# Moving each chunk's down projection ahead of the next drive in a fused scan and feed-forward kernel, with new budgets for the scan steps

## Chip, cores, metric

One core of one Trainium2 chip. The metric is device time in microseconds; "span" is the time from the first to the last traced instruction of the core, and it is a little shorter than the time. The granted TensorE clock is the share of full speed that the throttle let through, mean over the span. The kernel before takes 190.05 us (median of four runs, 189.99 to 190.41).

Short names: PE is TensorE, DVE is VectorE, ACT is ScalarE, POOL is GpSimd.

## The reference

For 2048 tokens of width 448: a layernorm; a diagonal complex state-space recurrence on the normalized tokens (branch A); a gated feed-forward with 1792 hidden units (branch B); and a gated sum.

```python
xn = layernorm(x)
# A: Bu = xn @ B_bar;  h_t = Lam_bar * h_{t-1} + Bu_t;  s = 2 Re(h @ C^T) + xn * Dskip
# B: B(xn) = (silu(xn @ w_gate) * (xn @ w_up)) @ w_down
g = silu(B(xn))
out = x + s * g
```

## The kernel before

The tokens go in four chunks of 512. For a chunk q, PE runs four stages:

- **drive**: input products of the scan (`pb`), pairs of matmuls on half the rows each;
- **gate/up** (`gu`): seven steps of four accumulations, also half-row pairs;
- **down**: four groups of 14 full-row matmuls (`hd`), from the product tile `Vt`;
- **outputs** (`outs`): four groups of C times the state `H` (`y`), then on DVE the gate, the sum and the store.

All PSUM results take turns in eight banks. The scan of a chunk is 19 DVE steps (six rotations in, seven scans, six rotations back) and one ACT copy. They wait in a background queue, and `bg.run(budget)` lets some of them into DVE's program between other work:

```python
    def run(self, budget):
        self.credit = min(self.credit + budget, 2.0 * budget)
        while self.steps and self.credit > 0:
            _, cost, fn = self.steps.popleft()
            fn()
            self.credit -= cost
```

The order of stages at the end of the kernel before:

```python
    drive(1, 4.8)
    for q in range(NQ - 1):
        sg = []
        for j in range(TQ):
            sg.append(down(q, j))
            bg.run(2.2)
        bg.finish(q)
        for j in range(TQ):
            finish(q, j, out_sum(q, j), sg[j])
        if q + 2 < NQ:
            drive(q + 2, 4.0)
            # ...
            gu(q + 2, bg, 2.2 if last else 1.5, {...})   # layernorm of chunk q+3 rides along
    # ... the last chunk: down and outputs, the last tile in two halves
```

A gate/up step hands a notice through POOL between the two halves of each accumulation (`tell`), and the square root of the layernorm is a POOL power that runs between such notices (`run_power`).

Of the kernel before, what the change touches and what calls it, by code (L numbers as in the profile page):

```python
# [44 lines left out]
def kernel(  # L45
# [25 lines left out]
    NQ = L // W  # L71
# [325 lines left out]
    def bu_alloc(q):  # L397
        bu_of[q] = [
            work.tile([P, KT, W], BF16, name=f"bu_{c}") for c in ("re", "im")
        ]  # L400
# [37 lines left out]
    def bu(q, ns, packed=False):  # L438

        C1 = W // 2  # L440
        b0, b1 = bu_of[q]
        ns = [*ns, KF] if packed else ns
        for two in (ns[:2], ns[2:]):
            pairs = []
            for n in two:
                pb = [bank("pb") for _ in range(2)]
                if n < KF:
                    pairs.append([(pb[i][:], BT[:, :, block(m)], (0, W))
                                  for i, m in enumerate((n, KT + n))])
                else:  # L450
                    pairs.append([(pb[i][:, 0:C1], BT[:, :, block(KF)], (i * C1, i * C1 + C1))
                                  for i in range(2)])
            if pairs:
                sums(q, pairs)
            for n, pair in zip(two, pairs):
                for i in range(2):
                    to = bu_of[q][i][:, n, :] if n < KF else b0[:, KF, i * C1 : i * C1 + C1]
                    nc.scalar.activation(to, pair[i][0], ACT.Copy)  # L458
        if packed:
            turn_over(b1[:, KF, :], b0[:, KF, :])  # L460
# [8 lines left out]
    def ssm_steps(bg, q):  # L469
        T = {}  # L470

        def alloc():
            T["b"] = bu_of[q]
            T["e"] = [work.tile([P, KT - c, W], BF16, name=n, bufs=1)
                      for c, n in enumerate(("ere", "eim"))]
            T["t"] = work.tile([P, KT, W], BF16, name="tmp", bufs=1)
            T["h"] = H_of[q] = [work.tile([P, KT - c, W], BF16, name=n)
                                for c, n in enumerate(("H_re", "H_im"))]

        def of(z, n):  # L480
            z = T["t"] if z == "t" else T[z[0]][z[1]] if isinstance(z, tuple) else z
            return z[:, 0:n, :]

        def step(n, out, a, b, op):
            def run():
                if not T:
                    alloc()
                nc.vector.tensor_tensor(out=of(out, n), in0=of(a, n), in1=of(b, n), op=op)

            bg.add(q, 0.3 * n, run)  # L490

        def scan(k, c):
            init = 0.0 if q == 0 else H_of[q - 1][c][:, k, W - 1 : W]
            nc.vector.tensor_tensor_scan(  # L494
                out=T["b"][c][:, k, :], data0=rcol[:, k : k + 1].to_broadcast([P, W]),
                data1=T["e"][c][:, k, :], initial=init, op0=ALU.mult, op1=ALU.add,
            )

        b0, b1, e0, e1, h0, h1 = (z for n in "beh" for z in ((n, 0), (n, 1)))
        step(KT, e0, b0, CT, ALU.mult)  # L500
        step(KT, "t", b1, ST, ALU.mult)
        step(KT, e0, e0, "t", ALU.add)
        step(KF, e1, b1, CT, ALU.mult)
        step(KF, "t", b0, ST, ALU.mult)
        step(KF, e1, e1, "t", ALU.subtract)
        for k in range(KF, -1, -1):
            for c in range(2 if k < KF else 1):
                bg.add(q, 1.22, lambda k=k, c=c: scan(k, c))
        bg.add(q, 0.0, lambda: turn_over(T["b"][1][:, KF, :], T["b"][0][:, KF, :]))
        step(KF, h1, b1, CT, ALU.mult)  # L510
        step(KF, "t", b0, ST, ALU.mult)
        step(KF, h1, h1, "t", ALU.add)
        step(KT, h0, b0, CT, ALU.mult)
        step(KT, "t", b1, ST, ALU.mult)
        step(KT, h0, h0, "t", ALU.subtract)
# [14 lines left out]
    def gu(q, bg, budget, hooks={}, begun=None):  # L530

        Vt = big.tile([P, NF, W], BF16, name="Vt", tag="vt")
        Vt_of[q] = Vt
        for f0 in range(0, NF, GRP):
            n = min(GRP, NF - f0)
            gs = work.tile([P, GRP, W], BF16, name="gs")
            us = work.tile([P, GRP, W], BF16, name="us")
            for i in range(0, n, 2):
                fi = f0 + i
                if begun and fi == 0:  # L540
                    banks = begun
                else:
                    banks = gu_banks()
                    gu_matmuls(q, fi, banks, 0, W)
                for j, (gp_, up_) in enumerate(banks):
                    nc.scalar.activation(gs[:, i + j, :], gp_[:], ACT.Silu)  # L546
                    nc.scalar.activation(us[:, i + j, :], up_[:], ACT.Copy)  # L547
                for fn in hooks.get(fi // 2, ()):
                    fn()
                bg.run(budget)  # L550
            nc.vector.tensor_tensor(  # L551
                out=Vt[:, f0 : f0 + n, :], in0=gs[:, 0:n, :], in1=us[:, 0:n, :], op=ALU.mult
            )

    def down(q, j):

        hd = bank("hd")[:, 0:D]
        for fi in range(NF):
            nc.tensor.matmul(  # L559
                hd, lhsT=Vt_of[q][:, fi, j * P : (j + 1) * P], rhs=Wd[:, fi, :],  # L560
                start=(fi == 0), stop=(fi == NF - 1),
            )
        sg = work.tile([P, D], BF16, name="sg", bufs=TQ)
        nc.scalar.activation(sg[:], hd, ACT.Silu)  # L564
        return sg

    def out_sum(q, j, k0=0, k1=KT):

        y = bank("y")
        m = q * TQ + j  # L570
        c0, c1 = k0 * P, min(k1 * P, D)
        for n in range(NS):
            h = H_of[q][n // KT][:, n % KT, j * P : (j + 1) * P]
            nc.tensor.matmul(  # L574
                y[:, c0:c1], lhsT=h, rhs=C2[:, n, c0:c1], start=(n == 0), stop=(n == NS - 1)
            )
            if k0 <= n < k1:
                skip = 0 if n < KF else P - R
                s = blk(n).start
                nc.tensor.matmul(  # L580
                    y[:, s + skip : s + P], lhsT=xT[:, n, m * P : (m + 1) * P],
                    rhs=Dd[:, n, skip:P], start=False, stop=False,
                )
        return y[:, c0:c1]

    def finish(q, j, y, sg, eng=nc.sync, c0=0, c1=D):
        m = q * TQ + j
        of = dict(tag="scr_f") if c1 - c0 < D else dict(bufs=1)
        t = work.tile([P, c1 - c0], F32, name="t", **of)
        nc.vector.tensor_tensor(out=t[:], in0=y, in1=sg[:, c0:c1], op=ALU.mult)  # L590
        of = dict(tag="scr_a") if c1 - c0 < D else {}
        ob = work.tile([P, c1 - c0], BF16, name="ob", **of)
        nc.vector.tensor_tensor(out=ob[:], in0=t[:], in1=x_all[:, m, c0:c1], op=ALU.add)  # L593
        eng.dma_start(out=out2d[m * P : (m + 1) * P, c0:c1], in_=ob[:])
# [57 lines left out]
    def load_c():  # L652
# [9 lines left out]
        4: [on(params_trig), on(ssm_steps, bg, 0)],  # L662
        5: [on(params_out)],
    }, begun)
    gu(1, bg, 0.9, {
        1: stats(8, 9),
        2: [*stats(10, 11), *sqrt(2), on(c_weights, 0)],
# [2 lines left out]
        5: [*transposes(10, 11), on(c_weights, 3)],  # L670
    })

    def drive(q, budget):
        bu_alloc(q)
        bu(q, (0, 1, 2), True)
        ssm_steps(bg, q)
        bg.run(budget)

    drive(1, 4.8)
    for q in range(NQ - 1):  # L680
        sg = []
        for j in range(TQ):
            sg.append(down(q, j))
            bg.run(2.2)
        bg.finish(q)
        for j in range(TQ):
            finish(q, j, out_sum(q, j), sg[j])
        if q + 2 < NQ:
            drive(q + 2, 4.0)
            n = (q + 3) * TQ  # L690
            last = q + 3 == NQ
            gu(q + 2, bg, 2.2 if last else 1.5, {} if last else {
                0: stats(n, n + 1),
                1: stats(n + 2, n + 3) + sqrt(q + 3),
                2: rstd_of(q + 3) + norms(n, n + 1),
                3: norms(n + 2, n + 3) + transposes(n, n + 1),
                4: transposes(n + 2, n + 3),
            })
    q, last = NQ - 1, TQ - 1
    bg.finish(q)  # L700
    sg = [down(q, j) for j in range(last)]
    for j in range(last):
        finish(q, j, out_sum(q, j), sg[j])
    sg = down(q, last)
    for k0, k1, eng in ((0, 2, nc.sync), (2, KT, nc.scalar)):
        finish(q, last, out_sum(q, last, k0, k1), sg, eng, k0 * P, min(k1 * P, D))
# [1 line left out]
_INS = ['A_x', 'A_Lambda_re', 'A_Lambda_im', 'A_B_re', 'A_B_im', 'A_C_re', 'A_C_im', 'A_log_dt', 'A_Dskip', 'B_x', 'B_w_gate', 'B_w_up', 'B_w_down']  # L708
_OUTS = [((1, 2048, 448), 'bfloat16')]
# [25 lines left out]
```

## Time and profile before

| | |
|---|---|
| time | 190.05 us |
| span | 188.1 us |
| PE busy | 182.1 us (97%) |
| DVE busy | 160.3 us (85%) |
| ACT busy | 105.1 us (56%) |
| chain that ended last | 84% PE |

The lines themselves stand in the prediction below. The two questions to put to them are whether PE streams at its rate or only looks busy, and which engine makes it wait.

### The profile page before, as it was taken

The numbers are of one execution on the slowest core, as the hardware profiler recorded it, in microseconds if no ns is written. First come the engines' busy times: TensorE is split into PE (matmuls) and PEld (weight loads), VectorE is DVE, ScalarE is ACT, GpSimd is POOL, SyncE is SP. The second block draws the span as 40 slices with busy tenths as digits, with TensorE's granted clock in tenths as the row PEclk, the third lists the DMA queues.
The fourth block names the chain that finished last, engine by engine and source line by source line (L and its number), as shares of the span: only waits on it lengthen the run. The fifth ranks groups of instructions, "written<-read, shape, count | busy, mean of one in ns | idle before, by whom it ended". The sixth has DMA issues, their size and how long they took to land.

```text
span 188.1 us, 3787 instructions
## 1 busy us (share of the span) xinstructions
PE 182.1 (97%) x1512; PEld 93.9 (50%) x1512; DVE 160.3 (85%) x266; ACT 105.1 (56%) x201; POOL 11.2 (6%) x21
## 2 busy tenths in 40 slices
PE   7799999999999999999999999999999999999992
PEld 2575455555555555545444455545444445555551
DVE  4889995899999999989999899789369999789253
ACT  3278699939999871018878632108977552302100
POOL 6422100000020000000020000000000000000000
PEclk9999999999999999999999999999999999999999
DMA  5999997300012100011004000020000000020020
GB/s 152 340 378 383 378 177 144 74 3 2 3 28 56 31 0 0 0 54 51 0 3 97 14 3 0 3 84 15 2 0 3 0 0 0 3 73 24 0 78 24
DMA packets 21122, 12.61 MB, mean 67 GB/s; under 512 B 11120, under 2 KB 20080, under 8 KB 21104
## 3 DMA queue, kind: packets, MB, share of 16 engines
q1 hardware_dynamic: 20288, 12.05, 23.2%
q10 hardware_dynamic: 688, 0.31, 0.6%
q8 instruction: 12, 0.20, 0.5%
q14 instruction: 6, 0.05, 0.1%
q0 software_dynamic: 128, 0.00, 0.0%
HBM read 8.03 MB, written 1.84 MB: 52 GB/s over the span
## 4 chain that ended last, share of the span: by engine, by line
PE 84%; DVE 9%; ACT 3%; DMA 1%; issue 1%; POOL 0%; SPq 0%; DVEq 0%
PE hd L559 23%; PE gp L424 20%; PE up L424 19%; PE y L574 11%; PE pb L424 9%; PE y L580 2%; DVE st L230 1%; DMA x_all<-in_A_x_dram 1%; DVE xn L248 1%; DVE f L356 1%; DVE a L357 1%; ACT CT L306 1%; DVE Vt L551 1%; ACT bu_im L458 1%; ACT bu_re L458 1%; DVE mv L231 1%
## 5 line engine op out<-in xcount | busy, mean ns | idle before, releaser
L424 PE MATMUL gp<-xT,Wg 64*128 64x512 bf16 (+1 forms) x406 | 86.2, 369 | 0.1
L424 PE MATMUL up<-xT,Wu 64*128 64x512 bf16 (+1 forms) x406 | 85.8, 369 | 0.1
L424 PEld LDWEIGHTS <-Wg 64*128 64x128 bf16 x406 | 36.9, 94 | 23.0 <-issue 1.6
L424 PEld LDWEIGHTS <-Wu 64*128 64x128 bf16 x406 | 37.2, 94 | 20.1 <-POOLq L406 0.3
L559 PE MATMUL hd<-Wd,Vt 128*128 128x448 bf16 x224 | 43.2, 353 | 0.0
L546 ACT ACTIVATE gs<-gp 128x512 bf16<-128x512 f32 x56 | 34.9, 623 | 12.4 <-PE gp L424 9.0
L547 ACT ACTIVATE us<-up 128x512 bf16<-128x512 f32 x56 | 35.2, 629 | 0.0
L559 PEld LDWEIGHTS <-Vt 128*128 128x128 bf16 x224 | 21.7, 98 | 21.0 <-issue 1.1
L564 ACT ACTIVATE sg<-hd 128x448 bf16<-128x448 f32 x16 | 8.7, 544 | 38.2 <-PE hd L559 38.2
L424 PE MATMUL pb<-xT,BT 64*128 64x512 bf16 (+1 forms) x224 | 22.0, 349 | 0.0
L551 DVE TENSOR_TENSOR Vt<-gs,us 128x2048 bf16<-128x2048 bf16 (+1 forms) x16 | 17.3, 1081 | 5.5 <-ACT us L547 5.4
L458 ACT ACTIVATE bu_re<-pb 128x512 bf16<-128x512 f32 (+1 forms) x20 | 10.0, 526 | 18.1 <-PE pb L424 18.1
L590 DVE TENSOR_TENSOR t<-y,sg 128x448 f32<-128x448 f32 (+2 forms) x17 | 10.1, 595 | 10.4 <-PE y L574 10.0
L574 PE MATMUL y<-C,H_re 128*128 128x448 bf16 (+2 forms) x68 | 17.6, 341 | 0.0
L424 PEld LDWEIGHTS <-BT 64*128 64x128 bf16 x224 | 11.2, 94 | 11.0 <-issue 0.7
L494 DVE TENSOR_TENSOR_SCAN bu_re<-rcol,H_re,ere 128x512 bf16<-128x512 f32 x12 | 15.1, 1269 | 0.0
L580 PE MATMUL y<-Dd,xT 128*128 128x128 bf16 x64 | 13.5, 212 | 0.0
L574 PE MATMUL y<-C,H_im 128*128 128x448 bf16 (+2 forms) x51 | 11.9, 342 | 0.0
L494 DVE TENSOR_TENSOR_SCAN bu_im<-rcol,H_im,eim 128x512 bf16<-128x512 f32 x9 | 11.3, 1260 | 0.0
L230 DVE BATCH_NORM_STATS2 st<-x_all 128x6 f32<-128x448 bf16 x16 | 9.9, 616 | 1.6 <-DMA x_all<-in_A_x_dram 1.5
L593 DVE TENSOR_TENSOR ob<-t,x_all 128x448 bf16<-128x448 f32 (+2 forms) x17 | 10.2, 597 | 0.6
L215 POOL TENSOR_TENSOR sd<-vep,halves 128x1 bf16<-128x1 bf16 (+1 forms) x7 | 5.9, 845 | 77.0 <-PE up L424 41.6
(90 smaller groups left out, 166.6 us busy)
## 6 DMA issues: line engine op xcount, KB each, us to landing
out_dram<-ob SPq DMA_DIRECT2D x15, 112.0 KB, 1.7
Wd<-in_B_w_down_dram SPq DMA_DIRECT2D x1, 1568.0 KB, 12.6
x_all<-in_A_x_dram SPq DMA_DIRECT2D x1, 896.0 KB, 14.5
Wg<-in_B_w_gate_dram SPq DMA_DIRECT2D x1, 768.0 KB, 8.2
Wu<-in_B_w_up_dram SPq DMA_DIRECT2D x1, 768.0 KB, 9.3
x_all<-in_A_x_dram SPq DMA_DIRECT2D x1, 448.0 KB, 5.1
Wg<-in_B_w_gate_dram SPq DMA_DIRECT2D x1, 384.0 KB, 4.9
Wu<-in_B_w_up_dram SPq DMA_DIRECT2D x1, 384.0 KB, 5.1
```

The source lines that it names most:

```text
L230: nc.vector.bn_stats(out=st[:], in_=x_all[:, n, :])
L424: mm = nc.tensor.matmul(out, lhsT=w[h, d, :], rhs=xT[h, d, q * W + c0 : q * W + c1], start=(first and m == 0), stop=(not first and m == 3 ...
L458: nc.scalar.activation(to, pair[i][0], ACT.Copy)
L494: nc.vector.tensor_tensor_scan(out=T["b"][c][:, k, :], data0=rcol[:, k : k + 1].to_broadcast([P, W]), data1=T["e"][c][:, k, :], initial=in ...
L546: nc.scalar.activation(gs[:, i + j, :], gp_[:], ACT.Silu)
L547: nc.scalar.activation(us[:, i + j, :], up_[:], ACT.Copy)
L551: nc.vector.tensor_tensor(out=Vt[:, f0 : f0 + n, :], in0=gs[:, 0:n, :], in1=us[:, 0:n, :], op=ALU.mult)
L559: nc.tensor.matmul(hd, lhsT=Vt_of[q][:, fi, j * P : (j + 1) * P], rhs=Wd[:, fi, :], start=(fi == 0), stop=(fi == NF - 1),)
L574: nc.tensor.matmul(y[:, c0:c1], lhsT=h, rhs=C2[:, n, c0:c1], start=(n == 0), stop=(n == NS - 1))
L580: nc.tensor.matmul(y[:, s + skip : s + P], lhsT=xT[:, n, m * P : (m + 1) * P], rhs=Dd[:, n, skip:P], start=False, stop=False,)
L590: nc.vector.tensor_tensor(out=t[:], in0=y, in1=sg[:, c0:c1], op=ALU.mult)
L593: nc.vector.tensor_tensor(out=ob[:], in0=t[:], in1=x_all[:, m, c0:c1], op=ALU.add)
```

## The change

The intent is to give DVE more regular work: the down projection of chunk q+1 runs right behind the outputs of chunk q, and the drive and gate/up of chunk q+2 come after it. The budgets are set anew. `downs(q, b)` is the four down groups of chunk q with `bg.run(b)` behind each, `outs` the four output groups (these helpers, which only wrap the loops, are cut).

```diff
     drive(1, 4.8)
-    for q in range(NQ - 1):
-        sg = []
-        for j in range(TQ):
-            sg.append(down(q, j))
-            bg.run(2.2)
-        bg.finish(q)
-        for j in range(TQ):
-            finish(q, j, out_sum(q, j), sg[j])
-        if q + 2 < NQ:
-            drive(q + 2, 4.0)
-            # ...
-            gu(q + 2, bg, 2.2 if last else 1.5, {...})
+    sg = downs(0, 2.2)
+    bg.finish(0)
+    outs(0, sg)
+    sg = downs(1, 2.5)
+    drive(2, 4.8)
+    gu(2, bg, 1.6, {...})
+    bg.finish(1)
+    outs(1, sg)
+    sg = downs(2, 2.5)
+    drive(3, 4.8)
+    gu(3, bg, 2.3)
+    bg.finish(2)
+    outs(2, sg)
     # ... the last chunk: three down groups (now with bg.run(2.5)), outputs, last tile
```

More of the change, by code (lines that the diff above doesn't have):

```diff
@@ L664, with drive, downs, outs @@
     }, begun)
+    def drive(q, budget):
+        bu_alloc(q)
+        bu(q, (0, 1, 2), True)
+        ssm_steps(bg, q)
+        bg.run(budget)
+    def downs(q, budget, hooks={}, n=TQ):
+        sg = []
+        for j in range(n):
+            sg.append(down(q, j))
+            for fn in hooks.get(j, ()):
+                fn()
+            bg.run(budget)
+        return sg
+    def outs(q, sg, hooks={}):
+        for j in range(len(sg)):
+            finish(q, j, out_sum(q, j), sg[j])
+            for fn in hooks.get(j, ()):
+                fn()
+    def do(fns):
+        for fn in fns:
+            fn()
     gu(1, bg, 0.9, {
@@ L671 @@
     })
-    def drive(q, budget):
-        bu_alloc(q)
-        bu(q, (0, 1, 2), True)
-        ssm_steps(bg, q)
-        bg.run(budget)
-    drive(1, 4.8)
-    for q in range(NQ - 1):
-        sg = []
-        for j in range(TQ):
-            sg.append(down(q, j))
-            bg.run(2.2)
-        bg.finish(q)
-        for j in range(TQ):
-            finish(q, j, out_sum(q, j), sg[j])
-        if q + 2 < NQ:
-            drive(q + 2, 4.0)
-            n = (q + 3) * TQ
-            last = q + 3 == NQ
-            gu(q + 2, bg, 2.2 if last else 1.5, {} if last else {
-                0: stats(n, n + 1),
-                1: stats(n + 2, n + 3) + sqrt(q + 3),
-                2: rstd_of(q + 3) + norms(n, n + 1),
-                3: norms(n + 2, n + 3) + transposes(n, n + 1),
-                4: transposes(n + 2, n + 3),
-            })
-    q, last = NQ - 1, TQ - 1
-    bg.finish(q)
-    sg = [down(q, j) for j in range(last)]
-    for j in range(last):
-        finish(q, j, out_sum(q, j), sg[j])
-    sg = down(q, last)
+    drive(1, 4.8)
+    sg = downs(0, 2.2)
[3 more added lines that the diff above has]
+    drive(2, 4.8)
+    gu(2, bg, 1.6, {
+        0: stats(12, 13),
+        1: stats(14, 15) + sqrt(3),
+        2: rstd_of(3) + norms(12, 13),
+        3: norms(14, 15) + transposes(12, 13),
+        4: transposes(14, 15),
+    })
+    bg.finish(1)
[5 more added lines that the diff above has]
+    outs(2, sg)
+    last = TQ - 1
+    sg = downs(3, 2.5, n=last)
+    bg.finish(3)
+    outs(3, sg)
+    sg = down(3, last)
     for k0, k1, eng in ((0, 2, nc.sync), (2, KT, nc.scalar)):
-        finish(q, last, out_sum(q, last, k0, k1), sg, eng, k0 * P, min(k1 * P, D))
+        finish(3, last, out_sum(3, last, k0, k1), sg, eng, k0 * P, min(k1 * P, D))
 _INS = ['A_x', 'A_Lambda_re', 'A_Lambda_im', 'A_B_re', 'A_B_im', 'A_C_re', 'A_C_im', 'A_log_dt', 'A_Dskip', 'B_x', 'B_w_gate', 'B_w_up', 'B_w_down']
```

## The prediction

> **What bounds the kernel now.** I read the page first (busy shares, the chain that ended last), then the busy time by stage with the stage limits set at the first matmul of each stage, then the waits of TensorE and VectorE from 60 us on, then the two engines' timelines.
>
> The page says that TensorE (PE) is busy 97% of the span and that 84% of the ending chain is on it:
>
> ```profile
> span 188.1 us, 3787 instructions
> PE 182.1 (97%) x1512; PEld 93.9 (50%) x1512; DVE 160.3 (85%) x266; ACT 105.1 (56%) x201; POOL 11.2 (6%) x21
> PE 84%; DVE 9%; ACT 3%; DMA 1%; issue 1%; POOL 0%; SPq 0%; DVEq 0%
> ```
>
> A busy PE need not be a PE at its rate, so I went to the timeline for the starts. Inside the gate/up stage the starts of a concurrent pair are 0.215 us apart (150.23, 150.45, 150.66); the five hd matmuls that start at 150.97 take 1.12 us with a last one of 0.35, so (1.12 - 0.35)/4 = 0.19 us apart. Only at the change of kind is a step longer: 150.66 to 150.97 is 0.31, so about 0.1 us is lost there.
>
> ```profile
> 150.23 0.38 PE L424 MATMUL up<-xT,Wu 64*128 64x512 bf16 x1
> 150.23 0.38 PE L424 MATMUL gp<-xT,Wg 64*128 64x512 bf16 x1
> 150.44 0.38 PE L424 MATMUL up<-xT,Wu 64*128 64x512 bf16 x1
> 150.45 0.38 PE L424 MATMUL gp<-xT,Wg 64*128 64x512 bf16 x1
> 150.66 0.38 PE L424 MATMUL up<-xT,Wu 64*128 64x512 bf16 x1
> 150.66 0.38 PE L424 MATMUL gp<-xT,Wg 64*128 64x512 bf16 x1
> 150.97 1.12 PE L559 MATMUL hd<-Wd,Vt 128*128 128x448 bf16 x5
> ```
>
> The stages (first column: from and to; then length; then busy time per engine) show in order: down projections of chunk 0, outputs of 0, drive (pb) of 2, gate/up of 2, down of 1, outputs of 1, drive of 3, gate/up of 3, down of 2, outputs of 2:
>
> ```profile
> 64.30:74.90 10.60, 10.60 (x58) 5.49 (x57) 10.50 (x12) 5.56 (x11) 0.00 (x0) 1.00 0.01 2
> 74.90:81.08 6.18, 6.18 (x45) 3.43 (x45) 6.06 (x7) 0.54 (x1) 0.00 (x0) 1.00 0.00 0
> 81.08:86.39 5.31, 5.31 (x58) 2.74 (x59) 4.86 (x7) 2.19 (x5) 0.00 (x0) 1.00 0.23 71
> 86.39:107.63 21.24, 21.24 (x200) 9.44 (x194) 20.36 (x36) 16.95 (x34) 1.24 (x1) 1.00 0.14 31
> 107.63:118.24 10.61, 10.61 (x59) 5.50 (x58) 10.54 (x11) 3.16 (x7) 0.00 (x0) 1.00 0.01 2
> 118.24:124.42 6.18, 6.18 (x46) 3.43 (x45) 4.44 (x7) 0.54 (x1) 0.00 (x0) 1.00 0.11 37
> 124.42:129.72 5.30, 5.30 (x57) 2.74 (x58) 5.11 (x6) 2.19 (x5) 0.00 (x0) 1.00 0.13 43
> 129.72:150.97 21.25, 21.25 (x200) 9.45 (x195) 16.20 (x16) 16.96 (x34) 0.00 (x0) 1.00 0.01 2
> 150.97:161.57 10.60, 10.60 (x58) 5.49 (x57) 10.56 (x11) 3.16 (x7) 0.00 (x0) 1.00 0.01 2
> 161.57:167.66 6.09, 6.09 (x46) 3.52 (x45) 4.47 (x7) 1.80 (x3) 0.00 (x0) 1.00 0.11 38
> ```
>
> Both gate/up stages last 98 pairs x 0.2155 = 21.12 us plus the 0.1 us of a change of kind; both down stages 56 x 0.189 = 10.58 us. That is the streaming time and nothing else. From 60 us on the waits of PE list is empty, and VectorE (DVE) is the one that waits:
>
> ```profile
> DVE t L590 <- PE y L574: 10.0, 12, 3.8
> DVE Vt L551 <- ACT us L547: 5.4, 3, 4.6
> ```
>
> So the middle of this kernel is one gapless stream on PE, and DVE, though over 95% busy in six of these ten stages, never makes it wait.
>
> **What the Trainium skill says.** (1) "TensorE: Matmul & The Clock Gate", Part 1, the section on 56 against 53.3 ns: start to start of a warm matmul is N / 2.4 GHz plus about 2.5 ns, 215.7 ns at N = 512. The trace agrees (0.2155 per pair of 512, 0.189 per 448 columns). There is then no issue slack for an order of matmuls to win. (2) "Perfetto Trace Analysis", Identifying the Most-Contended Engine: matmul busy time is no good measure of distance to roofline; hence the starts above. Here they confirm the busy share. (3) The same page, Matmuls (Optimizing Tensor Performance): independent groups should rotate through PSUM banks so that evacuation overlaps. The kernel rotates eight banks, and the trace shows no matmul held for one; whether it stays so is the first thing the new order could upset. (4) "VectorE: DVE Perf Modes", the perf-mode tier table: a bf16 tensor_tensor of 2048 takes 1224 ns; the trace has 1218 to 1225.
>
> **The change part by part.** No matmul, copy, scan step or transfer is added or removed. Three things move.
>
> *PE order.* Before, with D, O, B, G for down, outputs, drive, gate/up: B1 D0 O0 B2 G2 D1 O1 B3 G3 D2 O2 D3 O3. After: B1 D0 O0 D1 B2 G2 O1 D2 B3 G3 O2 D3 O3. D1 jumps ahead of B2 and G2, D2 ahead of B3 and G3. The sum of stage lengths is the same. Changes of kind between half-row pairs (B, G) and full-row matmuls (D, O), at 0.1 us: before B1-D0, O0-B2, G2-D1, O1-B3, G3-D2, five; after B1-D0, D1-B2, G2-O1, D2-B3, G3-O2, five. Net 0.0 us. If PE stays gapless: D1 from 81.0, B2 91.6, G2 96.9, O1 118.2, D2 124.3, B3 134.8, G3 140.1, O2 161.5, D3 167.6. Each O starts where it did.
>
> *Scan steps.* I replayed the credits of the background queue by hand, for the order that DVE gets. The steps of chunk 1 end in drive 2, those of chunk 2 in the fourth down of chunk 2, those of chunk 3 in the last gate/up pair. A step costs DVE, start to start in its timeline, about 1.18 us (four blocks or a scan) or 0.92 (three blocks): six of 1.18, six of 0.92, seven scans, 7.1 + 5.5 + 8.3 = 20.9 us a chunk. Now the two deadlines:
> - Chunk 2, for O1 and D2. After O0's last output (85.2) come six scans and six more steps of chunk 1, 7.1 + 6.3, to 98.6. From then to the end of G2 DVE has 6.3 (three steps of each size) + 5.9 (five scans) + 4.0 (Vt products, 3 x 1.14 + 0.6) + 5.9 of layernorm (four stats at 0.92, reciprocal and norms 2.2), 22.1, to 120.7. D2 reads the last Vt only after 124.3: margin 3.6. H of chunk 1 is there 20 us before O1.
> - Chunk 3 is the tight one, because its drive ends 10.4 us later. In the old trace the bu tile was whole 6.8 us after the drive began (87.24 + 0.67 - 81.08); so 134.8 + 6.8 = 141.6. DVE, done with chunk 2 at about 134.6, idles to there (7 us), then has 20.9 + 4.0 of Vt = 24.9 to do, to 166.5. H of chunk 3 is ready at 166, needed by O3 at 175.6: margin 9 (it was 2 in the old trace: 172.4 + 1.2 against 175.6). But the last Vt, queued behind the steps, lands at about 166.5 against D3 at 167.6: margin 1.1, and the outputs of O2 are finished late, to 171.5, where the banks they hold are not wanted before 177.
>
> *ScalarE.* The turn-over copies (1.27 us) move from inside G to the down stages for chunks 1 and 2, and to the fifth pair of G3 for chunk 3. ACT has 3.02 - 2.07 = 0.95 us idle per pair, so there it lags by 0.3, or about 0.9 if it waits for the last scan; the bank it frees late is wanted 2 to 3 us later.
>
> Also the last 3.7 us (outputs, 1.7 us of store) are untouched. Sum: PE 0.0, DVE 0.0 on the path, ACT 0.0: **190.0 us**.
>
> **Rivals.**
> - *DVE becomes the bound in the third gate/up.* Vt products are in line behind scan steps; gs has two buffers, so pair 4 waits for the first product (I have it at 152.6, wanted at about 153.9) and pair 6 for the second (158.5 against 159.9). For it: margins of 1.3 us, DVE busy to the last tenth there. Against: PSUM holds one more pair, another 1 us of cushion. If DVE is 2 to 3 us later than I have it, PE stalls 0.5 to 1.5 us: 190.5 to 191.5.
> - *The square-root power on GpSimd in G2.* The power waits for DVE's statistics and stands ahead of the notices that let the second half of a pair begin. I have statistics done at 104.9, power 0.85 more, next notice wanted at 107.8: margin 2. If lost, 0.5 to 1 us: about 190.8.
> - *A gain:* D1 between O0 and B2 gives the y banks 10 us to be freed, where before drive 2 followed at once. But no wait on a bank shows in the old trace, so there is nothing to win; the best case is a change of kind or two less, 189.8. A gain of 2% would need 3.8 us, and the only PE time not streaming is in the first 12 us and the last 4, both untouched.
>
> **Range and chances.** Runs before spread over 0.4 us. A gain has room for 0.2 to 0.3; a stall of up to 1 us is possible at three places with margins near 1 to 2 us. So 189.5 to 191.0. Faster by 2%: 0.01; slower by 2% (193.8) needs two or three stalls together: 0.03; within: 0.96.
>
> **What would show it.** Right: the stage lengths above in the new order, O1 at 118.2, O2 at 161.5, an empty PE wait list after 60 us; DVE idle about 7 us before its first step of chunk 3, then busy to about 166; H of chunk 3 done 9 us before O3. Wrong: a PE wait on the Vt product at D3, on a bank in G2 or G3, or on GpSimd in G2; or PE starts in the new order closer or wider than 0.2155 and 0.189 us.

## The result

The changed kernel takes **189.69 us** (189.64 to 189.77, four runs) against 190.05 before. The ratio is 0.9978, with a 95% interval of 0.996 to 0.9995. Ratios here are the mean time of one kernel's fast runs over that of the other's of the same rounds, so not quite the ratio of the medians. That is inside the predicted range and 0.3 us under the predicted time.

The head of the page of the changed kernel (busy us, share and count of each engine; then the chain that ended last by engine):

```profile
span 187.9 us, 3793 instructions
PE 182.4 (97%) x1512; PEld 94.4 (50%) x1512; DVE 159.9 (85%) x266; ACT 105.0 (56%) x201; POOL 11.9 (6%) x21
PE 84%; DVE 9%; ACT 3%; DMA 1%; issue 1%; POOL 0%; DVEq 0%
```

The stages of the changed kernel, in the same columns as in the prediction (from:to, length, then the busy time of PE, weight loads, DVE, ACT and POOL). In order: down 0, outputs 0, down 1, drive 2, gate/up 2, outputs 1, down 2, drive 3, gate/up 3, outputs 2.

```profile
64.19:74.79 10.60, 10.60 (x58) 5.49 (x57) 10.50 (x12) 5.56 (x11) 0.00 (x0) 1.00 0.01 2
74.79:80.88 6.09, 6.09 (x46) 3.52 (x45) 6.02 (x7) 0.54 (x1) 0.00 (x0) 1.00 0.00 0
80.88:91.57 10.69, 10.69 (x59) 5.39 (x57) 9.49 (x12) 1.63 (x3) 0.00 (x0) 1.00 0.14 44
91.57:96.87 5.30, 5.30 (x57) 2.73 (x58) 5.23 (x7) 3.98 (x8) 0.00 (x0) 1.00 0.01 2
96.87:118.12 21.25, 21.25 (x200) 9.45 (x195) 20.91 (x36) 15.70 (x32) 1.92 (x1) 1.00 0.13 27
118.12:124.22 6.10, 6.10 (x47) 3.54 (x46) 5.82 (x9) 1.53 (x4) 0.00 (x0) 1.00 0.06 19
124.22:134.90 10.68, 10.68 (x57) 5.38 (x55) 10.40 (x12) 2.89 (x5) 0.00 (x0) 1.00 0.11 35
134.90:140.21 5.31, 5.31 (x57) 2.74 (x58) 0.45 (x1) 2.73 (x6) 0.00 (x0) 1.00 0.00 0
140.21:161.46 21.25, 21.25 (x201) 9.45 (x195) 19.52 (x19) 16.96 (x34) 0.00 (x0) 1.00 0.01 2
161.46:167.55 6.09, 6.09 (x46) 3.53 (x45) 6.05 (x8) 1.52 (x4) 0.00 (x0) 1.00 0.00 0
```

Every stage has its old length to 0.1 us. Outputs lose 0.1 us where full-row matmuls now follow, and down stages gain 0.1 us where half-row pairs now follow. From the start of down 0 to the start of the last half-tile's outputs PE needs 182.81 - 64.30 = 118.51 us before and 182.71 - 64.19 = 118.52 us after. **On PE the change is worth nothing.** The waits of the changed kernel from 60 us on (engine, line, releaser: us in total, times, longest) have no PE line; DVE's are these:

```profile
DVE t L590 <- PE y L574: 8.0, 4, 5.3
DVE ere L488 <- ACT bu_re L458: 6.4, 1, 6.4
DVE ob L593 <- DMA out_dram<-ob: 0.7, 1, 0.7
```

DVE's idle time has moved (before the drive of chunk 3 is copied out, and before the last outputs) but is still nobody's loss. Three lines of its timeline, for chunk 3: the first scan step, the last one (the state `H_re` is whole), and the last product:

```profile
141.76 1.22 DVE L488 TENSOR_TENSOR ere<-bu_re,CT 128x2048 bf16<-128x2048 bf16 x1 [6.41 <-ACT bu_re L458]
164.83 1.21 DVE L488 TENSOR_TENSOR H_re<-H_re,tmp 128x2048 bf16<-128x2048 bf16 x1
165.97 0.68 DVE L551 TENSOR_TENSOR Vt<-gs,us 128x1024 bf16<-128x1024 bf16 x1
```

So where do 0.36 us come from? The trace begins 0.1 us earlier at the first transpose (5.43 against 5.53 us), ahead of every changed line; over all the traces that start varies between 5.34 and 5.58 whatever the kernel. The rest lies outside the span: each run lists its time and its core's span. Time minus span is 1.74 to 1.82 us in the four runs of the changed kernel. In the profiled run of the kernel before it is 190.19 - 188.1 = 2.09. (Spans of single runs are to 0.1 us, so each such remainder is good to 0.05.)

### The profile page after: what moved, and what is told of

It is laid out like the page before. It is cut to its first block, busy times and chain, and to the rows that moved or that the text cites. A ratio compares the mean times of both kernels' runs of the same rounds, so it can differ in the third digit from the quotient of the medians.

```text
span 187.9 us, 3793 instructions
## 1 busy us (share of the span) xinstructions
PE 182.4 (97%) x1512; PEld 94.4 (50%) x1512; DVE 159.9 (85%) x266; ACT 105.0 (56%) x201; POOL 11.9 (6%) x21
## 3 DMA queue, kind: packets, MB, share of 16 engines
HBM read 8.03 MB, written 1.84 MB: 52 GB/s over the span
## 4 chain that ended last, share of the span: by engine, by line
PE 84%; DVE 9%; ACT 3%; DMA 1%; issue 1%; POOL 0%; DVEq 0%
PE hd L559 23%; PE gp L424 20%; PE up L424 19%; PE y L574 11%; PE pb L424 9%; DVE st L230 2%; PE y L580 2%; DVE xn L248 1%; DMA x_all<-in_A_x_dram 1%; DVE f L356 1%; DVE a L357 1%; ACT CT L306 1%; DVE mv L231 1%; DVE Vt L551 1%; ACT bu_im L458 1%; ACT bu_re L458 1%
## 5 line engine op out<-in xcount | busy, mean ns | idle before, releaser
L559 PEld LDWEIGHTS <-Vt 128*128 128x128 bf16 x224 | 21.8, 98 | 20.5 <-issue 0.2
L488 DVE TENSOR_TENSOR ere<-bu_re,CT 128x2048 bf16<-128x2048 bf16 x4 | 4.9, 1221 | 8.9 <-ACT bu_re L458 6.4
L215 POOL TENSOR_TENSOR sd<-vep,halves 128x1 bf16<-128x1 bf16 (+1 forms) x7 | 6.6, 941 | 87.9 <-DVE vep L232 86.0
```

The costliest lines, as they stand in the source:

```text
L559: nc.tensor.matmul(hd, lhsT=Vt_of[q][:, fi, j * P : (j + 1) * P], rhs=Wd[:, fi, :], start=(fi == 0), stop=(fi == NF - 1),)
```

## The experiments

Theory A: PE is one gapless stream in either order; nothing is won on the path, and the 0.3 us come from something beside it. Theory B: the new order or pace itself wins some tenths. The rivals of the prediction (DVE late in the third gate/up, the POOL power late in the second) were tested by making DVE late on purpose.

### Again, order alone, paces alone, one block (five rounds, one chip, one set of runs of the kernel before)

`k1_again` is the changed kernel unaltered.

> The changed kernel unaltered, to see whether the 0.36 us between the medians (190.05 to 189.69) is the change. Theory A (the new order wins nothing on the path; the difference sits ahead of the changed code): stage lengths on TensorE from 60 us on as in the first trace within 0.1 us, time 189.6 to 190.1, and the kernel before in the same rounds within 0.3 us of it. Theory B (the new order wins 0.2 to 0.4 us): the ratio stays at 0.998 with an interval clear of 1, and the first 60 us of both traces end at the same time.

`k2_order_only` keeps the new order with the old budgets:

```diff
-    sg = downs(1, 2.5)
-    drive(2, 4.8)
-    gu(2, bg, 1.6, {
+    sg = downs(1, 2.2)
+    drive(2, 4.0)
+    gu(2, bg, 1.5, {
# ... the same for chunk 3 (2.2, 4.0, 2.2), and bg.finish(3) ahead of the last downs
```

> The new order of down projections and drives with the old budgets of the scan steps (2.2, 4.0, 1.5, 2.2). A: 189.6 to 190.1, the same as the whole change, TensorE never waits after 60 us, some steps of chunk 3 left for the last down stage. B: it carries the whole gain if the order is what wins, and half or none of it if the paces do. A rival in which the paces were needed for the new order: over 190.5, with a TensorE wait on the scan of chunk 3.

`k3_paces_only` keeps the old order with the new budgets:

```diff
-            bg.run(2.2)
+            bg.run(2.5 if q else 2.2)
-            drive(q + 2, 4.0)
+            drive(q + 2, 4.8)
-            gu(q + 2, bg, 2.2 if last else 1.5, {} if last else {
+            gu(q + 2, bg, 2.3 if last else 1.6, {} if last else {
# ... and bg.run(2.5) between the last down groups
```

> The old order with the new budgets (2.5, 4.8, 1.6, 2.3). A: 189.8 to 190.3, as before, stage lengths as before. B with the paces as the winner: 189.7. Rival: the faster pace in the old order makes VectorE late for a product in the third gate/up, over 190.5.

`k8_one_block` takes the reordering further, with one block of half-row stages:

```diff
     gu(2, bg, 1.6, {...})
+    drive(3, 4.8)
+    gu(3, bg, 2.3)
     bg.finish(1)
     outs(1, sg)
     sg = downs(2, 2.5)
-    drive(3, 4.8)
-    gu(3, bg, 2.3)
     bg.finish(2)
```

> A further reordering: gate/up of 2, drive of 3 and gate/up of 3 stand in one block, so that half-row and full-row matmuls change over three times after 60 us, not five. If a change-over costs 0.1 us each and nothing else bounds, TensorE's stream ends 0.2 us earlier relative to 60 us than in the changed kernel: 189.5. If VectorE cannot take chunk 3 so early beside chunk 2 and the layernorm (its bu comes at about 125 us, with about 45 us of work to the outputs of chunk 1 at 145), a TensorE wait shows and it is 190 to 192.

Measured (the last column is the range over all runs of that kernel; the column before it is PE's time from the start of down 0 to the outputs of the last half-tile, in the profiled run):

| kernel | median us | ratio to before (95%) | PE 64 to 183 us | time - span, us |
|---|---|---|---|---|
| before, 11 runs | 190.11 | | 118.51 | 2.09 to 2.21 |
| k1_again | 189.83 | 0.9979 (0.9967 to 0.9991) | 118.52 | 1.78 to 1.83 |
| k2_order_only | 189.84 | 0.9983 (0.997 to 0.9996) | 118.51 | 1.75 to 1.83 |
| k3_paces_only | 190.11 | 0.9999 (0.9985 to 1.0012) | 118.52 | 2.15 to 2.21 |
| k8_one_block | 189.52 | 0.9969 (0.9955 to 0.9983) | 118.31 | 1.74 to 1.82 |

The gain is real and goes with the order, not the paces: by its ratio, B as I had put it would seem right. But in the trace A is right: the PE stream is 118.5 us in all four kernels that have five changes of kind, and the median spans are 187.9 to 188.1 us. The whole gain is in time minus span.

The one-block order does win on PE, by what the prediction took for a change of kind. Where gate/up 2 runs into drive 3, the step keeps its pace, and where it runs into the outputs of chunk 1 it doesn't. The two timelines (start, length, instruction), changed kernel first:

```profile
117.81 0.38 PE L424 MATMUL up<-xT,Wu 64*128 64x512 bf16 x1
117.81 0.38 PE L424 MATMUL gp<-xT,Wg 64*128 64x512 bf16 x1
118.12 0.36 PE L574 MATMUL y<-C,H_re 128*128 128x448 bf16 x1
```

```profile
117.53 0.38 PE L424 MATMUL up<-xT,Wu 64*128 64x512 bf16 x1
117.54 0.38 PE L424 MATMUL gp<-xT,Wg 64*128 64x512 bf16 x1
117.75 0.38 PE L424 MATMUL up<-xT,Wu 64*128 64x512 bf16 x1
117.75 0.38 PE L424 MATMUL gp<-xT,Wg 64*128 64x512 bf16 x1
117.97 1.03 PE L424 MATMUL pb<-xT,BT 64*128 64x512 bf16 x8
```

118.12 - 117.81 = 0.31 us against 117.97 - 117.75 = 0.22. Two changes of kind fewer save 118.52 - 118.31 = 0.21 us. DVE took the earlier chunk 3 without making PE wait, so the feared 190 to 192 us did not come. This version beats the kernel before by 0.3%. Over the changed one it is 0.1%, and the two intervals overlap: there it is the 0.21 us of PE's stream that carries the point.

### DVE late on purpose (one round, two runs each)

Spare multiplies of 128 x 1792, written into a dead buffer, delay what stands behind them on DVE. The results stay correct.

```diff
+    def idle_work(n):
+        for _ in range(n):
+            nc.vector.tensor_tensor(out=natC[:, 0], in0=CT[:, :, 0:D], in1=ST[:, :, 0:D], op=ALU.mult)
# k4_late_vt2, k5_late_vt5, k6_late_g3:
-    gu(3, bg, 2.3)
+    gu(3, bg, 2.3, {6: [on(idle_work, 2)]})   # k4;  k5: {6: ... 5};  k6: {0: ... 3}
# k7_late_stats, in gu(2, ...):
-        1: stats(14, 15) + sqrt(3),
+        1: [on(idle_work, 3)] + stats(14, 15) + sqrt(3),
```

> The changed kernel with two spare VectorE multiplies (about 1.05 us each) ahead of the last step and the last Vt product of chunk 3: that product ends at about 168.7 in place of 166.6, where the down projection of chunk 3 starts at 167.55. If the first down matmul waits for the whole Vt tile (as my margin of 1.1 us assumed): a stall of about 1.1 us at 167.5, time plus 1.1. If each matmul waits only for its own group of Vt (the last group is read by the 13th matmul, at 169.8): no stall, plus 0.0.

> Five spare multiplies there: the last product ends at about 171.9. Waiting for the whole tile: plus about 4.3 us. Waiting for its own group: plus about 2.1 us, with the stall between the 12th and 13th matmul of the first down group. If VectorE did not matter at all: plus 0.

> Three spare multiplies (3.2 us) in the first pair of the third gate/up, so that VectorE is later from there on, as in the first rival of the prediction. By that rival TensorE stalls 0.5 to 1.5 us; worked out anew from the trace after: pairs do not stall (bank of pair 4 free at 158.2, wanted at 158.3), but the turn-over copy on ScalarE waits for the last scan to 160.8 and holds up the fifth pair's copies, so the first output matmul of chunk 2 waits for its bank about 1.2 us. Whole-tile wait on Vt at the down projection would add about 1.0.

> Three spare multiplies (3.2 us) ahead of the last two statistics in the second gate/up, as in the second rival: the square-root power on GpSimd then ends at about 109.4 and the notice behind it, for the second half of the fourth pair (wanted at 107.7), is late: a stall of about 1.7 to 1.9 us in the fourth pair, time plus 1.8. If GpSimd's queue is no obstacle: plus 0.0.

In these rounds the changed kernel did not run beside them, so the figure to compare with its 118.52 us is PE's time from the start of down 0 to the last half-tile's outputs: k4 118.52, k5 122.60, k6 118.54, k7 120.12.

**k4** took 190.15 us. The last Vt product ended at 168.92 (168.24 + 0.68), 1.2 us after the down projection had begun, and PE's timeline shows no gap: 22 steps in 4.51 - 0.35 us are 0.189 each.

```profile
167.69 4.51 PE L559 MATMUL hd<-Wd,Vt 128*128 128x448 bf16 x23
```

A down matmul waits for its own group of Vt only. The tight margin of the prediction (1.1 us) was taken to the first matmul; to the thirteenth, which reads the last group, it is 12 x 0.189 = 2.3 us more, 3.4 in all (3.2 by the measured times of the changed kernel).

**k5** took 193.74 and 192.44 us, on average 1.0147 (1.006 to 1.0234) times the kernel before. The first of these was profiled. PE's timeline shows the stall where the second reading puts it, behind the twelfth matmul, and it lasts 2.2 us as expected. But the down stage is 12.03 us in place of 7.95, so 4.1 us longer:

```profile
167.48 2.43 PE L559 MATMUL hd<-Wd,Vt 128*128 128x448 bf16 x12
172.13 4.13 PE L559 MATMUL hd<-Wd,Vt 128*128 128x448 bf16 x12 [2.22 <-DVE Vt L551]
```

After the stall twelve matmuls take 4.13 us, so on average (4.13 - 0.35)/11 = 0.34 us a step, not 0.19. The busy table by stretch tells why (the granted clock is the third number from the right):

```profile
170.00:172.00 2.00, 0.00 (x0) 0.00 (x0) 2.00 (x4) 0.00 (x0) 0.00 (x0) 1.00 0.00 0
172.00:174.00 2.00, 1.87 (x6) 0.78 (x7) 1.86 (x4) 0.54 (x1) 0.00 (x0) 0.55 0.00 0
174.00:176.00 2.00, 2.00 (x8) 0.88 (x7) 1.83 (x3) 0.00 (x0) 0.00 (x0) 0.59 0.35 115
176.00:180.00 4.00, 4.00 (x25) 2.08 (x24) 1.29 (x3) 0.84 (x2) 0.00 (x0) 1.00 0.18 57
```

The clock was granted at 0.55 and 0.59 right after the gap (the same view of 172.22 to 175.63 gives 0.50). In this run a wait of 2.2 us on PE cost another 1.7 to 1.9 us of slow matmuls. It is no fixed price: the other run of the same kernel, of which no trace is kept, has a clock of 1.000 and a span of 190.6 us. That is 1.4 less than in the profiled run and 2.7 more than the 187.9 of the changed kernel, so nearer to the wait alone. What made the difference is not shown.

**k6** took 189.95 us with DVE 3.1 us later through the whole third gate/up. ACT waited for the Vt product, and PE did not wait at all: gate/up 3 is 21.25 us and the down stage 7.97.

```profile
ACT gs L546 <- DVE Vt L551: 2.6, 2, 2.2
```

Neither the 0.5 to 1.5 us of the prediction's first rival nor the 1.2 us that I worked out for this run came. The turn-over copy (ACT's copy of one scan result with its halves swapped) started at 158.17, before the last scan ended (159.45 + 1.25 = 160.7), so it waits for the first scan alone. That ACT's 1 us of idle time per pair and the spare PSUM pair took up the rest is my reckoning; no run takes them apart. The last Vt product ended at 169.69 (169.01 + 0.68), and the thirteenth down matmul was due at 167.47 + 2.27 = 169.74: the margin at the down projection was just used up.

**k7** took 191.49 us, 1.0063 (1.003 to 1.0097). Gate/up 2 is 22.85 us in place of 21.25, and the wait list of PE holds one line:

```profile
PE up L424 <- POOLq L406: 1.4, 1, 1.4
```

PE resumed at 109.19, 0.1 us after the statistics were done (108.92 + 0.16), where POOL records the start of the power (such records on POOL are rough):

```profile
109.15 1.92 POOL L215 TENSOR_TENSOR sd<-vep,halves 128x4 bf16<-128x4 bf16 x1 [56.41 <-DVE vep L232]
```

The stall cost 1.6 us where 1.7 to 1.9 were expected. So the second rival is a real mechanism: a power in POOL's queue that waits for DVE holds the notices behind it. In the changed kernel the statistics are done at 105.35 and the notice is wanted at about 107.7, a margin of 2.3 us against the 2 predicted.

### What holds the 0.35 us outside the span

The first runs left a remainder that the trace's views do not cover. Counted in the traces' records, the new order holds six more semaphore instructions, five on ACT and one on DVE. Three runs add tiny instructions to the **kernel before**, behind its first outputs, where ACT idles and DVE keeps nobody waiting:

```diff
+        if q == 0:
+            for _ in range(5):                                            # k9_act5, k11_both
+                nc.scalar.activation(silu_of[:], half_pi[:], ACT.Copy)    # k9_act5, k11_both
+            nc.vector.memset(den[:], 0.0)                                 # k10_dve1, k11_both
         if q + 2 < NQ:
             drive(q + 2, 4.0)
```

> The kernel before with five tiny ScalarE copies (one column each) added where ScalarE idles, after the first outputs. In the runs so far the span from first to last instruction is the same for both orders (187.9 to 188.1), and the gain of 0.35 us lies in time minus span: 2.1 to 2.2 us with the old order, 1.75 to 1.83 with the new. The new order's ScalarE stream holds five more semaphore instructions. If the length of ScalarE's stream sets that remainder: time minus span falls to 1.8 and the time to about 189.8. If not: 2.15 and 190.1. TensorE stages unchanged either way.

> The kernel before with one tiny VectorE memset added at that place (the new order's VectorE stream holds one more instruction). If VectorE's stream length sets the remainder: time minus span 1.8, time about 189.8. If not: 2.15 and 190.1.

> Both additions. If the remainder goes by the lengths of the two streams together, it becomes 1.8 here alone. If it stays 2.15 in all three, the remainder goes with something of the new order that these runs do not name, and its cause stays open.

One run goes the other way: the **changed kernel** with one set-up memset moved from DVE to POOL.

```diff
-        nc.vector.memset(two_pi[h], v)
+        (nc.vector if v > 0 else nc.gpsimd).memset(two_pi[h], v)
```

> The changed kernel with one tiny set-up memset moved from VectorE to GpSimd, so that VectorE's traced stream holds 312 instructions as in the kernel before, the new order and paces kept. If the gain of the change is only that its VectorE stream is one instruction longer (one added memset gave the kernel before the same gain): time minus span goes back to 2.15 and the time to about 190.1 to 190.2, as before. If the new order itself is also worth something there: it stays at 1.8 and 189.8. TensorE stages after 60 us unchanged either way.

| kernel | order | DVE records | ACT records | median us | ratio to before (95%) | time - span, us |
|---|---|---|---|---|---|---|
| before | old | 312 | 228 | 190.16 | | 2.11 to 2.29 |
| k9_act5 | old | 312 | 233 | 190.09 | 0.9997 (0.9985 to 1.001) | 2.10 to 2.24 |
| k10_dve1 | old | 313 | 228 | 189.83 | 0.9986 (0.9972 to 0.9999) | 1.73 to 1.92 |
| k11_both | old | 313 | 233 | 189.73 | 0.9979 (0.9966 to 0.9991) | 1.74 to 1.91 |
| k12_dve_less1 | new | 312 | 234 | 190.08 | 1.0002 (0.999 to 1.0014) | 2.10 to 2.18 |

One tiny memset on DVE gives the old order the remainder of the new one (with 0.14% by the ratio of k10, 0.21% by that of k11, against 0.22% for the change; the intervals overlap), and taking one DVE instruction from the new order takes the gain away. PE's stages are unchanged in all of them. (The before runs beside k12 have a median of 190.13; one of them, at 192.16, has a span of 190.0 and an ordinary remainder of 2.16.)

Two limits. k12 also lengthens POOL's and ACT's streams by a little, so it is the pair of k10 and k12 that carries the point, not k12 alone. And the rule is not "longer is better": with 315 and 316 DVE records (k4, k6, k7; two runs each) the remainder was 1.91 to 2.09, with 318 (k5) 1.74 and 1.84. What the chip does there, before the first or after the last traced instruction, no view shows; it stays open.

## Why the prediction was right

- **"PE order ... Net 0.0 us" held.** The stream is 118.52 us against 118.51. O1 began at 118.12 (predicted 118.2), O2 at 161.46 (161.5). Five changes of kind cost as much as five. That one costs 0.1 us, read from a single step of the old trace, was confirmed by k8, which saved two and 0.21 us.
- **"Scan steps" held nearly to the tenth for chunk 3, to 0.7 us for chunk 2.** DVE began chunk 3 at 141.76 after 6.4 idle us (predicted 141.6 and 7), ended its last Vt product at 166.65 (166.5), and had H of chunk 3 at 166.04 (166). Chunk 2 ran later than predicted: its last Vt product ended at 121.23 (120.7) and its last step at 135.34 (134.6). A wait of 0.7 us for a store (`ob`), which the prediction did not have, is in it. The idle time before chunk 3 hid that. Working with start-to-start steps from the old timeline helped: the durations overlap, and with them the 20.9 us of a chunk would have been 6 x 1.22 + 6 x 0.95 + 7 x 1.26 = 21.8.
- **The margin at D3 was mis-sized.** "The last Vt ... lands at about 166.5 against D3 at 167.6: margin 1.1" assumed that the first down matmul needs the last group. k4 and k5 show that the thirteenth does, which makes it 3.4, or 3.2 by the measured times (166.65 against 167.55 + 2.27). This made the upper end of the range wider than it had to be.
- **The first rival was mis-sized.** "If DVE is 2 to 3 us later than I have it, PE stalls 0.5 to 1.5 us": k6 made it 3.1 us later and PE stalled 0.0. In the changed kernel the first product was there at 152.94 and its buffer wanted at 154.88, a margin of 1.9 us and not 1.3; and in k6 ACT began that pair 1.2 us late (156.08) without PE feeling it, so the cushion behind it is at least that and not 1.
- **The second rival was right in mechanism; that its margin came out (2.3 us against 2) is luck.** The statistics were done at 105.35 and not at 104.9, but the "power 0.85 more" did not count, since in k7 PE resumed 0.1 us after the statistics: two errors that nearly cancel. k7 shows the price, 1.6 us for statistics that are 3.7 us later (3.3 us of multiplies and what they shifted).
- **"ScalarE" held.** The turn-over copy of chunk 3 started at 156.97, before the last scan ended (157.66), so the case "if it waits for the last scan" did not come, and no PE wait followed.
- **The gain of 0.35 us was in no term of the sum.** The prediction gave a possible gain of 0.2 to 0.3 us to fewer changes of kind; that was not the cause. It goes with the DVE program being one traced instruction longer, a by-product of the new order, and lies outside the span; why it does so is open. The range had no term for it; that 0.35 us still fitted in is luck.

## What to carry to other kernels

When the bound engine starts its instructions at its streaming rate with no wait in the list, an order of stages can only win what its changes of kind cost; count those before anything else. Before crediting a gain of some tenths of a microsecond to a design, take the span from the time, run by run, and try a change that does nothing at the same place. A lag of an engine off the path costs nothing until its margin is gone, and where the bound engine then idled for 2.2 us, a lower clock cost nearly as much again in one of two runs.

## What the Trainium skill lacked or had wrong

- "Runtime: NRT & Kernel Launch", The ~15µs preamble/postamble breakdown, speaks of a kernel-invariant gap between a profile's total and the reported time. That is not the same pair of numbers as here, but time minus span in these runs is not invariant: 2.09 to 2.29 us with 312 DVE records and 1.73 to 1.92 with 313, in either order. With 315 to 318 it is not in step with the count. No page that I read ties it to the length of an engine's program.
- "TensorE: Matmul & The Clock Gate", Part 1, What's actually happening, puts the half clock after at least one idle window of about 3.4 us. In the profiled run of k5 an idle stretch of 2.2 us was followed by a granted clock of 0.50 over 3.4 us; the other run of k5 kept a mean clock of 1.000, and in k7 a stretch of 1.4 us was followed by no lower clock.
- "TensorEngine Tiling (Array Packing)", Key Properties, names a drain at a change of tiling mode but no time for it. The price of changing between half-row pairs and full-row matmuls was 0.09 to 0.1 us per change here, 0.21 us for two.
- No page that I read says whether a notice in POOL's queue waits for the power ahead of it to end. In k7 the power is recorded from 109.15 for 1.92 us, yet PE, which needed the notice behind it, resumed at 109.19. So the notice waited for the power's start and not for its end, if POOL's record is right.
